# Seven PSUM banks of an attention loop in one ring, taken by a written rank, and another written order for the quads with an output piece

## The chip, the cores and the metric

One core of one Trainium2 chip runs the whole program. The metric is the device time in microseconds (us) of one execution: the median of the runs.

## The reference

A transformer block on 2048 tokens of width 576: multi-query attention with 32 heads of 18 columns that share one K and one V, then an MLP, each behind a LayerNorm with modulation. What the change touches is the attention:

```python
q = (x @ wq).reshape(B, S, H, Dh).transpose(0, 2, 1, 3)   # H = 32, Dh = 18, S = 2048
k = x @ wk                                                # one head, shared
v = x @ wv
scores = einsum("bhqd,bkd->bhqk", q, k) * (Dh ** -0.5)
p = softmax(scores, axis=-1)
o = einsum("bhqk,bkd->bhqd", p, v)
out = o.transpose(0, 2, 1, 3).reshape(B, S, H * Dh) @ wo
```

## The kernel before

The attention is worked in 32 quads (the loop over `n` at the end of the printed code): four heads and 512 tokens each. TensorE, VectorE and ScalarE each run a list of instructions in order; which instruction comes when is written out by hand in the strings `QUAD` (quads 0 to 8) and `QUADW` (quads 9 to 30), one token per step. Quad 31 has an order of its own made from `LAST` and `LASTW`. The tokens:

- `S0`, `S1`: a score matmul (`st_mm`, L931), 512 columns, from the upper (0) or lower (1) 64 rows of the array. It fills one PSUM bank; ScalarE's exp (L933) empties it into `P`. 64 a quad.
- `M0`, `M1`: a matmul (`smax_mm`, L319) whose bank VectorE empties with a maximum (L953), 48 a quad; these prepare the softmax's shift for the quad after. `X1` (L941, emptied by ScalarE's Relu at L944) and `R1` (L319 again, emptied by VectorE at L951) work in pairs, 8 each a quad. So a quad has 128 banks to fill and empty.
- `V1` to `V4`: so many 128-column pieces of P times V (`pv_mm`, L921), with 32 columns of weights in four column tiles; they run eight chunks behind the exps and add up in the one bank `psC`. 64 pieces a quad. What stands between two `V` tokens is called a burst here.
- `F1`, `F2` (`smax_fin1`, `smax_fin2`, L349 to L366): the next quad's maxima are reduced, transposed on TensorE (L357), copied by ScalarE (L359) and VectorE (L360), and written by four DMAs (L364) from SP's queue into the rows of the next quad's `QST` that its score matmuls read: the first two DMAs into the rows of `S0`, the last two into those of `S1`.
- `T1`, `RC`, `T2`, `OS`: the steps of `post_quad` for the quad before. `WO`: one piece of the output projection (`wo_piece`, L723, 14 matmuls of 288 columns) whose bank VectorE adds to `XT` (L727); in eight of the quads five transposes (L155) follow it.

The eight PSUM banks of this stage (`open_ps("2", 4)`) are split by the names `psM` (three banks, taken in turn by M and R), `psB` (four, taken in turn by S, X, F2, WO and the transposes) and `psC` (one). A matmul that takes a bank waits until the engine that reads it has emptied it. The last quads let odd `S` steps take `psM` as well. Two matmuls that follow each other on different row halves start together:

```python
QUADW = """M1 M1 S0 S0 X1 S1 M0 V4 S1 M0 S1 S0 M1 M0 V4 ..."""
t = ps()                                  # st_mm: psB, or psM in the last quads
t = psM()                                 # mx_mm, M and R
```

Of the kernel before, what the change touches and what calls it, by code (L numbers as in the profile page):

```python
# [8 lines left out]
F32 = mybir.dt.float32  # L9
# [11 lines left out]
NQT = NB * NQ  # L21
# [11 lines left out]
def block_kernel(ctx: ExitStack, tc, x, wqkv, wo, w1, b1, w2, b2, c, wmod, ident_in, out):  # L33
# [7 lines left out]
    PS = {}  # L41

    def open_ps(stage, b):

        if PS:
            PS["pool"].__exit__(None, None, None)
        PS["pool"] = tc.tile_pool(name="ps" + stage, bufs=1, space=bass.MemoryType.PSUM,
                                  **({"reuse_waits": "tile"} if PS else {}))
        PS["t"], PS["b"] = PS["pool"].__enter__(), b

    def psA(): return PS["t"].tile([128, 2, 512], F32, name="psA", bufs=2)
    def psM(): return PS["t"].tile([128, 512], F32, name="psM", bufs=3)
    def psB(): return PS["t"].tile([128, 512], F32, name="psB", bufs=PS["b"])
    def psC(): return PS["t"].tile([128, 512], F32, name="psC", bufs=1)

    open_ps("1", 3)
    def big(): return per.tile([128, 10, 512], F32R, name="big", bufs=3)
# [26 lines left out]
    V = pa.tile([128, S // 128, 32], F32, name="V")  # L84
# [267 lines left out]
            ve.tensor_reduce(m[:, :8], mm[:, :8, :], axis=AX.X, op=ALU.max)  # L352
            ve.tensor_reduce(m[:, 8:], mm[:, 8:, :3], axis=AX.X, op=ALU.max)

    def smax_fin2(n):
        p = psB()
        pe.transpose(p[:16, :128], MR.pop(n), ident)  # L357
        ms = pa.tile([16, 2, 128], F32R, name="ms")
        ac.activation(ms[:, 0], p[:16, :128], AF.Copy, scale=-1.0)  # L359
        ve.scalar_tensor_tensor(ms[:, 1], p[:16, :128], -1.0, ms[:, 0].bitcast(F32), op0=ALU.mult, op1=ALU.subtract)  # L360
        for g in range(2):
            for s in range(2):
                r = 64 * g + R3 + s
                sy.dma_start(QST[n][r:r + 1].rearrange("o p (t c) -> o (p t) c", c=128).bitcast(F32),  # L364
                             ms[8 * g:8 * (g + 1), s].bitcast(F32))
# [80 lines left out]
    for tb in range(NB):  # L446
        nz = big() if tb + 1 < NB else None
        for i, m in enumerate((4, 0, 1, 2, 3)):
# [27 lines left out]
            if tb < 2:  # L476
                for _ in range(NSTAT[tb][i]):
                    ln1_stats(*stats.popleft())
                for _ in range(NAPPLY[tb][i]):
                    b, t = applies.popleft()  # L480
# [3 lines left out]
    load_q(2)  # L484
    ph1.__exit__(None, None, None)
    open_ps("2", 4)
    psM(), psC()
    pxp = tc.tile_pool(name="px", bufs=1, reuse_waits="tile")
    px = pxp.__enter__()
    a2 = tc.tile_pool(name="a2", bufs=1, side="right", reuse_waits="tile")  # L490
# [238 lines left out]
    def wo_piece(tb, t, h2, p):  # L729
        wo_mm(tb, t, h2, p, 0, KD)  # L730
        wo_add(tb, t, h2, p)
# [137 lines left out]
    def tail_parts(o, tail, d, e=po):  # L869

        e.tensor_tensor(d, tail[:, 0], tail[:, 1], op=ALU.subtract)
        for x, y in ((o[:, :2], tail), (o[:, 2], d)):
# [8 lines left out]


    LAG = 8
    QUAD = """S0 M0 S1 S1 M0 V3 S0 M1 S1 M0 M1 S0 V3 M0 S1 M1 S0 V2 M0 S1 S1 M0 X1 S0 V4 T1 X1 M0 M1 M0 S1 S0
            V4 S1 RC M0 S1 S0 M0 S0 M1 V3 S0 M1 R1 S1 S0 M0 X1 V3 M0 S1 S1 R1 S0 M0 S1 V3 M0 X1 M0 S0 S1 S0
            M1 V3 M0 S1 S1 M0 S0 R1 S0 V3 R1 S0 S1 M1 S0 M0 X1 V3 M0 S1 M0 S1 S0 S0 R1 V3 M0 X1 S0 M1 S0 M1
            V3 S1 M0 M0 S1 T2 S0 S1 V4 M0 S1 S0 M1 S0 M1 V3 S0 R1 S1 M0 F1 S1 S0 V3 X1 M0 S1 M0 R1 S0 F2 OS
            V4 M0 M1 S0 S1 M0 X1 V4 S1 M0 S1 S0 M1 M0 S1 V2 R1 S0 M1 S0 V2 S0 S1 M0 M1 V2 S1""".split()
    QUADW = """M1 M1 S0 S0 X1 S1 M0 V4 S1 M0 S1 S0 M1 M0 V4 M0 S1 S0 M0 S1 T1 M0 X1 V4 S1 RC S0 S0 M1 M0 S1 V4
            S0 R1 M1 S0 S1 M0 S1 V3 S1 M0 S0 X1 M0 M0 S1 V2 M0 S1 S0 R1 V2 M0 X1 M0 S1 S0 S1 M0 V4 S0 T2 R1  # L890
            M0 S1 OS S0 M1 WO S0 R1 M1 S0 M1 S0 X1 V3 S0 M1 M0 S1 S1 M1 S0 V3 M0 S1 S0 R1 S0 M0 X1 V3 M0 S1
            X1 M0 S1 M0 S1 V4 S1 M0 R1 S0 M1 S0 V4 S0 M1 M0 F1 S1 S0 S1 V4 M0 S1 M0 X1 S0 M1 F2 V4 M1 S0 S0
            S1 M0 S1 M0 V3 R1 S0 S0 S1 R1 M0 V3 S0 S1 M0 S1 M0 S1 V3 M0 S1 M1 S0 M1 S0 V3""".split()
    LASTW = "S0 S1 S0 S1 S0 S1 WO V4 S0 S1 V4".split()
    LAST = "S0 S1 S0 S1 V4 S0 S1 S0 S1 V4".split()
    P, PVt = {}, {}
# [27 lines left out]
            posts.append(post_quad(n, PVt.pop(n)))  # L924
            next(posts[0])

    def st_mm(n, kc, g, i, ps):
        if (n, kc) not in P:
            P[n, kc] = pb.tile([128, 4, TB], F32, name="P", bufs=4)
        t = ps()  # L930
        pe.matmul(t, KS[64 * g:64 * g + 64, 128 * kc:128 * (kc + 1)], QST[n][64 * g:64 * g + 64, i, :],  # L931
                  start=True, stop=True)
        ac.activation(P[n, kc][:, 2 * i + g, :], t, AF.Exp, scale=SCALE)  # L933

    XC = deque()

    def mx_mm(n, u, kb, what, g):
        p, qt = UNITS[u]
        if what == "X":
            t = psB()  # L940
            pe.matmul(t, QST[n][64 * g:64 * g + 64, p, 128 * qt:128 * (qt + 1)], KD1[64 * g:64 * g + 64, :],  # L941
                      start=True, stop=True)
            XC.append(pb.tile([128, 512], F32, name="xc", bufs=2))
            ac.activation(XC[-1], t, AF.Relu)  # L944
            return
        t = psM()
        o = mx_tile(n)[:, 8 * g + 4 * p + qt, (2 if what == "R" else kb):][:, :1]
        smax_mm(n, t, g, p, qt, 3 if what == "R" else kb)
        if what == "R":
            c = XC.popleft()  # L950
            ve.tensor_tensor_reduce(c, t, c, 1.0, -3.0e38, ALU.add, ALU.max, o)  # L951
        else:
            ve.tensor_reduce(o, t, axis=AX.X, op=ALU.max)  # L953
# [13 lines left out]

    pieces = deque((tb, t, h2) for tb in range(NB - 1) for t in range(NT) for h2 in range(2))

    def wo_next(ps):  # L970
        tb, t, h2 = pieces.popleft()
        wo_piece(tb, t, h2, ps())
        for _ in range(2):
            if held[0] == "T":
                held[0] = step(fill)
        if h2 and tb < 2:
            fill.append(ln2_rows(tb, t))

    pq = 0
    for n in range(NQT):  # L980
        ns = [0, 0]
        if n < NQT - 1:
            order = QUADW if n > NQ else QUAD
            if n == NQT - 2:
                order = order + ["WO"]
        else:
            order = []
            for d in range(8):
                order += LASTW + ["RW"] if d == 4 else LAST
                order += {1: ["T1"], 2: ["RC"], 4: ["T2"], 5: ["OS", "V4"]}.get(d, [])  # L990
        if n < NQT - 1:
            kf, kr = (sum(int(tok[1]) for tok in order[:order.index(a)] if tok[0] == "V") // 4 for a in ("F2", "RC"))
            quiet = kf - 2, kf - 1, kr - 1
        for tok in order:
            if tok[0] == "V":
                g = int(tok[1])
                while g:
                    i = min(g, 4 - pq % 4)
                    if pq >= LAG:
                        pv_mm(*divmod((pq - LAG) // 4, 16), pq % 4, pq % 4 + i)  # L1000
                    pq, g = pq + i, g - i
                    if pq % 4 == 0:
                        between(*divmod(pq // 4 - 1, 16))
            elif tok[0] == "S":
                g = int(tok[1])
                st_mm(n, ns[g] // 2, g, ns[g] % 2, psM if ns[g] % 2 and (n == NQT - 1 or n == NQT - 2 and ns[g] > 24) else psB)
                ns[g] += 1
            elif tok in maxima:
                unit = next(maxima[tok], None)
                if unit:  # L1010
                    mx_mm(*unit, tok[0], int(tok[1]))
            elif tok == "WO":
                wo_next(psB)
            elif tok == "RW":
                for i, w in enumerate("hl"):
                    sy.dma_start(WO[w][:, KD - 1, :].bitcast(F32), woscr[i])
            elif tok[0] == "F":
                (smax_fin1 if tok == "F1" else smax_fin2)(n + 1)
            elif n:
                if next(posts[0], 0) == 0:  # L1020
                    posts.pop()
        if n == NQT - 1:
            W1["r"] = per.tile([128, 40, 128], F32R, name="w1a", tag="big", bufs=3)
            load_w1(0, " ".join(OPS) + " tails")
# [13 lines left out]
    def op_pieces(R, e2):  # L1038


        at = {"B11": (0, 0, ve), "B21": (2, 2, e2), "B22": (4, 7, e2), "T2": (6, 5, ve), "T1": (8, 5, ve),
              "T3": (10, 0, ve), "T4": (12, 2, e2), "t0": (0, 4, ve), "t1": (1, 9, ve)}
        less = {"T3": (5, 0, 0), "T4": (2, 5, 2), "T1": (7, 5, 5)}

        def form(what):
            for w in what.split():
                if w[0] == "=":
                    x, y, o = (R[:, i:i + 2] for i in less[w[1:]])
                    (ve if w == "=T3" else e2).tensor_tensor(o, x, y, op=ALU.subtract)
# [455 lines left out]
```

## Time and profile before

| | us |
|---|---|
| median of 3 runs (lowest, highest) | 2227.75 (2227.24, 2228.18) |
| span of the profiled execution | 2225.7 |
| a quad of `QUAD`, from its first score matmul to the next quad's (quad 5) | 37.4 |
| a quad of `QUADW` without transposes (quad 11) | 39.25 |
| a quad of `QUADW` with transposes (quad 12) | 39.9 |
| busy in quad 11: TensorE, VectorE, ScalarE | 39.25, 37.9, 37.3 |

The span runs from the first to the last instruction of the profiled execution; the runs' time has some 2 us around it. The busy times are unions: an instruction's duration overlaps that of its neighbours on the same engine where they are pipelined, and a matmul's end is modelled, so TensorE counts as busy from one start to the next. How fast TensorE really goes is therefore read from the starts of its instructions.

### The profile page before, as it was taken

To read this page: it belongs to the slowest core of one execution; us is meant where nothing else is said; L and a number is where in the kernel's file an instruction comes from. 1 tells how busy PE (TensorE), PEld (TensorE's weight loads), DVE (VectorE), ACT (ScalarE), POOL (GpSimd) and SP (SyncE) were. 2 spreads that over 40 slices of the span, in tenths; PEclk is the share of its full clock that TensorE was granted. 3 is DMA by queue.
4 is the path that set the end of the run, shared out by engine and by line. 5 is a ranking of instruction groups with operands and counts; after the bars stand their busy time and mean duration, and the time that the engine had idled before them with its cause. 6 is when DMAs were issued, how large, how long until landed. Compare 5 with 4: busy or idle time off the path is not lost.

```text
span 2225.7 us, 46108 instructions
## 1 busy us (share of the span) xinstructions
PE 2207.4 (99%) x16630; PEld 1451.2 (65%) x16630; DVE 1931.9 (87%) x3415; ACT 1639.8 (74%) x3145; POOL 1527.0 (69%) x1761
## 2 busy tenths in 40 slices
PE   8999999999999999999999999999999999999999
PEld 6654544444544445454454545888888898989898
DVE  7589999999999999999999983887888878888887
ACT  5569999999999999999999997444444444343443
POOL 6653455666776687677676631888888867877776
PEclk9999999999999999999999999999999999999999
DMA  6232143433333333333333322666666646676664
GB/s 231 85 131 92 34 135 115 139 125 119 127 119 114 115 129 105 107 126 111 126 123 117 115 70 63 205 178 175 178 179 180 185 129 182 180 218 188 177 185 124
DMA packets 184776, 308.00 MB, mean 138 GB/s; under 512 B 19711, under 2 KB 75407, under 8 KB 184549
## 3 DMA queue, kind: packets, MB, share of 16 engines
q1 hardware_dynamic: 184405, 304.91, 44.3%
q8 instruction: 132, 2.16, 0.4%
q14 instruction: 95, 0.78, 0.1%
q10 hardware_dynamic: 144, 0.15, 0.0%
HBM read 200.97 MB, written 93.79 MB: 132 GB/s over the span
## 4 chain that ended last, share of the span: by engine, by line
PE 93%; ACT 1%; DVE 1%; issue 0%; ACTq 0%; DVEq 0%
PE psC L921 24%; PE psB L1144 18%; PE psA L1247 16%; PE psB L931 14%; PE psM L319 12%; PE psB L723 2%; PE psB L941 2%; PE psA L1281 1%; PE psA L723 1%; ACT P L933 1%; PE psB L155 0%; PE psB L248 0%; PE psB L357 0%; PE psM L931 0%; DVE mx L344 0%; DVE mx L337 0%
## 5 line engine op out<-in xcount | busy, mean ns | idle before, releaser
L933 ACT ACTIVATE P<-psB 128x512 f32<-128x512 f32 x2008 | 1051.1, 621 | 43.8 <-PE psM L319 20.0
L953 DVE TENSOR_REDUCE mx<-psM 128x1 f32<-128x512 f32 x1476 | 934.3, 682 | 29.9 <-PE psM L319 12.9
L931 PE MATMUL psB<-qst,KS 64*128 64x512 f32 x2008 | 603.5, 435 | 0.1
L319 PE MATMUL psM<-KS,qst 64*128 64x512 f32 x1722 | 591.2, 435 | 0.5 <-DVE mx L337 0.5
L921 PE MATMUL psC<-P,V 128*32 128x256 f32 (+3 forms) x6600 | 571.9, 440 | 0.5 <-ACT O L738 0.5
L931 PEld LDWEIGHTS psB<-qst,KS 64*128 64x128 f32 x2008 | 300.4, 184 | 225.6 <-ACT P L933 185.1
L319 PEld LDWEIGHTS psM<-KS,qst 64*128 64x128 f32 x1722 | 284.1, 184 | 185.6 <-DVE mx L953 130.2
L1144 PE MATMUL psB<-ops,w1a 128*128 128x512 f32 x1512 | 393.8, 396 | 0.2 <-DVE h L1159 0.2
L1144 PEld LDWEIGHTS psB<-ops,w1a 128*128 128x128 f32 x1512 | 270.1, 188 | 46.7 <-DVE h L1159 0.6
L921 PEld LDWEIGHTS psC<-P,V 128*32 128x32 f32 x6600 | 146.4, 108 | 185.3 <-issue 156.6
L1253 DVE TENSOR_TENSOR XT<-psA,XT 128x576 f32<-128x576 f32 x330 | 241.8, 753 | 18.6 <-PE psA L1247 13.2
L1247 PEld LDWEIGHTS psA<-w2s,big 128*128 128x128 f32 x1584 | 223.0, 188 | 14.0 <-POOL big L1221 2.5
L1247 PE MATMUL psA<-w2s,big 128*128 128x288 f32 x1584 | 230.5, 294 | 0.0
L1157 ACT ACTIVATE psB<-gs 128x512 f32<-128x512 f32 x144 | 86.7, 602 | 127.8 <-DVE gs L1156 127.7
L1221 POOL TENSOR_TENSOR big<-s,big 128x512 fp32r<-128x512 f32 x132 | 170.8, 1294 | 10.6
L951 DVE CUSTOM_DVE_ANT_0 xc<-psM,xc 128x512 f32<-128x512 f32 x246 | 166.3, 683 | 12.8 <-PE psB L931 6.4
L1153 ACT ACTIVATE h<-psB,b1t 128x512 f32<-128x512 f32 x144 | 97.9, 680 | 102.0 <-PE psB L1144 81.3
L758 POOL TENSOR_TENSOR os<-O,os 128x512 fp32r<-128x512 f32 x31 | 39.9, 1286 | 185.4 <-ACT os L757 185.4
L944 ACT ACTIVATE xc<-psB 128x512 f32<-128x512 f32 x246 | 154.7, 629 | 4.0 <-PE psB L941 1.4
L1156 DVE SCALAR_TENSOR_TENSOR gs<-psB,h 128x512 f32<-128x512 f32 x144 | 98.6, 685 | 39.8 <-ACT psB L1154 39.7
L792 POOL TENSOR_TENSOR r<-r,r 128x256 fp32r<-128x256 f32 (+1 forms) x162 | 121.8, 752 | 13.0
L1162 ACT ACTIVATE big<-h 128x512 fp32r<-128x512 f32 x39 | 24.7, 634 | 133.8 <-DVE h L1159 133.8
(212 smaller groups left out, 3326.8 us busy)
## 6 DMA issues: line engine op xcount, KB each, us to landing
w1a<-w1scr SPq DMA_DIRECT2D x252, 256.0 KB
w2s<-w2sum SPq DMA_DIRECT2D x132, 288.0 KB
w1scr<-r SPq DMA_DIRECT2D x126, 256.0 KB
w2s<-w2scr SPq DMA_DIRECT2D x76, 288.0 KB
w2scr<-r SPq DMA_DIRECT2D x72, 288.0 KB
w2sum<-r SPq DMA_DIRECT2D x72, 288.0 KB
qst<-qscr SPq DMA_DIRECT2D x192, 72.0 KB
w1a<-w2scr SPq DMA_DIRECT2D x33, 288.0 KB
```

The costliest lines, as they stand in the source:

```text
L319: pe.matmul(o, QST[n][64 * g:64 * g + 64, p, 128 * qt:128 * (qt + 1)], KS[64 * g:64 * g + 64, 512 * kb:512 * (kb + 1)], start=True, stop=True)
L792: po.tensor_tensor(o[:, n:2 * n], src, o[:, :n].bitcast(F32), op=ALU.subtract)
L921: pe.matmul(PVt[n][32 * j:32 * (j + 1), cs], V[:, kc, :], t[:, j, cs], start=(kc == 0 and h0 == 0), stop=(kc == 15), skip_group_check=True)
L931: pe.matmul(t, KS[64 * g:64 * g + 64, 128 * kc:128 * (kc + 1)], QST[n][64 * g:64 * g + 64, i, :], start=True, stop=True)
L933: ac.activation(P[n, kc][:, 2 * i + g, :], t, AF.Exp, scale=SCALE)
L944: ac.activation(XC[-1], t, AF.Relu)
L951: ve.tensor_tensor_reduce(c, t, c, 1.0, -3.0e38, ALU.add, ALU.max, o)
L953: ve.tensor_reduce(o, t, axis=AX.X, op=ALU.max)
L1144: pe.matmul(o, x, y, start=(first and i == 0), stop=(i == len(terms) - 1), skip_group_check=True)
L1221: po.tensor_tensor(unit(u, 1), x, unit(u, 0).bitcast(F32), op=ALU.subtract)
L1247: pe.matmul(p[:, i, :288], x[:, ts_], W2S[k][:, y], start=(bool(first) and q == 0), stop=(q == 2), skip_group_check=True)
L1253: ve.tensor_tensor(o, p[:, :, :288], o, op=ALU.add)
```

## The change

The three banks of `psM` and the four of `psB` become one list of seven, `RING`. A step takes the bank at place `rank` of that list, and the bank goes to the list's end; rank 0 is the bank that was taken longest ago. The rank stands in the order strings: `S0+` has rank 1, `X1++` rank 2. `psB()` outside of these steps takes rank 0 while the ring exists. In `QUAD` the tokens are the same and stand in the same order, with ranks added (34 plus signs); `QUADW` is another order of the same tokens, with 37.

```diff
-    def psB(): return PS["t"].tile([128, 512], F32, name="psB", bufs=PS["b"])
+    def psB(): return bank() if RING else PS["t"].tile([128, 512], F32, name="psB", bufs=PS["b"])
+    RING = []
+    def bank(rank=0):
+        b = RING.pop(rank)
+        RING.append(b)
+        return PS["t"].tile([128, 512], F32, name="bk%d" % b, bufs=1)
...
     open_ps("2", 4)
-    psM(), psC()
+    RING.extend(range(3))
+    bank(), bank(), bank(), psC()
+    RING[:] = 3, 0, 4, 1, 5, 2, 6
...
-    QUADW = """M1 M1 S0 S0 X1 S1 M0 V4 S1 M0 S1 S0 M1 M0 V4 M0 S1 S0 M0 S1 T1 M0 X1 V4 S1 RC S0 S0 M1 M0 S1 V4
-            S1 M0 S1 M0 V3 R1 S0 S0 S1 R1 M0 V3 S0 S1 M0 S1 M0 S1 V3 M0 S1 M1 S0 M1 S0 V3""".split()
+    QUADW = """S1+ M0 M0 X1 S0 X1 M0 V3 S1 M0 M0+ S1 R1 S0+ V2 M1 S0 M0 S1+ S0 R1+ V3 M0 X1+ S0 S1+ S0+ M1 V4 S0 T1
+            R1 M0+ F1 S1 S0 X1+ V4 M0 S1 M0 S1+ S0+ M1 F2 V3 S0+ R1 S0+ S1 M0 S1 M0 V3 M0 X1 S1 M0+ S1 R1+ S0 V3""".split()
...
-    def st_mm(n, kc, g, i, ps):
+    def st_mm(n, kc, g, i, rank):
-        t = ps()
+        t = bank(rank)
...
-            t = psB()
+            t = bank(rank)
-        t = psM()
+        t = bank(rank)
...
+            rank = tok.count("+")
+            tok = tok.rstrip("+")
-                st_mm(n, ns[g] // 2, g, ns[g] % 2, psM if ns[g] % 2 and (n == NQT - 1 or n == NQT - 2 and ns[g] > 24) else psB)
+                st_mm(n, ns[g] // 2, g, ns[g] % 2, rank)
...
     form = op_pieces(YR[0], ve)
+    RING.clear()
     open_ps("3", 4)
```

Counted over the strings, bursts and `V` tokens of a quad become (a burst that runs over the quad's end is counted whole; slots are starts, with two matmuls on different row halves in one):

| | bursts of 7 banks, 4 slots | of 6, 3 slots | of 4, 2 slots | V4 | V3 | V2 | after F2 to the quad's end |
|---|---|---|---|---|---|---|---|
| `QUAD`, both | 8 | 10 | 3 | 5 | 12 | 4 | |
| `QUADW` before | 10 | 9 | 1 | 9 | 8 | 2 | V4, 7, V3, 6, V3, 6, V3, 6, V3 |
| `QUADW` now | 8 | 12 | 0 | 8 | 10 | 1 | V3, 7, V3, 7, V3 |

Two places of TensorE's list show it. The first is where one quad of `QUADW` ends and the next begins (quads 27 and 28), with the semaphores that each waits for; L931 is a score matmul, L319 a maximum's, L921 P times V, and DMAHW a DMA queue's. Before:

```order
L921 MATMUL psC<-P,V 32x384 x4
L319 MATMUL psM<-KS,qst 128x512 [waits DVE_49] x2
L931 MATMUL psB<-qst,KS 128x512 [waits DMAHW7_49,DMAHW6_49,Activation_49]
L931 MATMUL psB<-qst,KS 128x512 [waits Activation_49]
L941 MATMUL psB<-KD_82,qst 128x512 [waits Activation_49]
L931 MATMUL psB<-qst,KS 128x512 [waits DMAHW1_49,DMAHW0_49,Activation_49]
```

Now (the lines have moved: L941 is the score matmul, L327 the maximum's, L951 the X, L931 P times V):

```order
L931 MATMUL psC<-P,V 32x384 x4
L941 MATMUL bk_18866<-qst,KS 128x512 [waits DMAHW2_49,DMAHW1_49,Activation_49]
L327 MATMUL bk_18869<-KS,qst 128x512 [waits DVE_49]
L327 MATMUL bk_18872<-KS,qst 128x512 [waits Activation_49]
L951 MATMUL bk_18875<-KD_82,qst 128x512 [waits DVE_49]
L941 MATMUL bk_18879<-qst,KS 128x512 [waits DMAHW7_49,DMAHW0_49,Activation_49]
```

The first score matmul of a quad was an `S0` that waits for the first two DMAs of L364; now it is an `S1` that waits for the last two, and it stands first in the quad. A score matmul may wait for VectorE now, and a maximum's for ScalarE.

The second place is in quad 5, inside `QUAD`, with the numbers of the tiles. Before:

```order
L319 MATMUL psM_4300<-KS_80,qst_3665 128x512 [waits DVE_49]
L931 MATMUL psB_4304<-qst_3076,KS_80 128x512 [waits Activation_49]
L931 MATMUL psB_4307<-qst_3076,KS_80 128x512 [waits Activation_49]
L319 MATMUL psM_4310<-KS_80,qst_3665 128x512 [waits DVE_49]
L941 MATMUL psB_4313<-KD1_82,qst_3665 128x512 [waits Activation_49]
L931 MATMUL psB_4317<-qst_3076,KS_80 128x512 [waits Activation_49]
```

Now:

```order
L327 MATMUL bk0_4302<-KS_80,qst_3667 128x512 [waits Activation_49]
L941 MATMUL bk6_4306<-qst_3078,KS_80 128x512 [waits Activation_49]
L941 MATMUL bk4_4309<-qst_3078,KS_80 128x512 [waits DVE_49]
L327 MATMUL bk1_4312<-KS_80,qst_3667 128x512 [waits Activation_49]
L951 MATMUL bk3_4315<-KD1_82,qst_3667 128x512 [waits DVE_49]
L941 MATMUL bk5_4319<-qst_3078,KS_80 128x512 [waits Activation_49]
```

The six steps are the same and stand in the same order; four of them take a bank that the other engine emptied.

## Rows read from the trace of the kernel before

**Rows 1.** The page, parts 1 and 4 (the chain that ended last).
```profile
PE 2207.4 (99%) x16630; PEld 1451.2 (65%) x16630; DVE 1931.9 (87%) x3415; ACT 1639.8 (74%) x3145; POOL 1527.0 (69%) x1761
...
PE 93%; ACT 1%; DVE 1%; issue 0%; ACTq 0%; DVEq 0%
```

**Rows 2.** Windows, quads 5, 11, 29: length; busy PE, PEld, DVE, ACT, POOL; clock.
```profile
318.51:355.90 37.39, 37.39 (x367) 18.51 (x363) 36.53 (x71) 36.99 (x76) 24.60 (x37) 1.00 0.41 133
...
547.67:586.92 39.25, 39.25 (x344) 19.17 (x345) 37.89 (x75) 37.30 (x76) 34.96 (x51) 1.00 0.36 122
...
1259.31:1298.57 39.26, 39.26 (x344) 19.27 (x345) 37.08 (x72) 37.29 (x76) 23.77 (x35) 1.00 0.34 116
```

**Rows 3.** Timeline, PE, quad 28: start, length, line, operation, tile, count.
```profile
1221.00 1.06 PE L921 MATMUL psC<-P,V 128*32 128x512 f32 x8
1221.99 0.49 PE L931 MATMUL psB<-qst,KS 64*128 64x512 f32 x1
...
1222.88 1.06 PE L921 MATMUL psC<-P,V 128*32 128x512 f32 x8
1223.88 0.50 PE L319 MATMUL psM<-KS,qst 64*128 64x512 f32 x1
...
1225.00 1.06 PE L921 MATMUL psC<-P,V 128*32 128x512 f32 x8
1225.99 0.73 PE L931 MATMUL psB<-qst,KS 64*128 64x512 f32 x3
1226.33 0.62 PE L319 MATMUL psM<-KS,qst 64*128 64x512 f32 x2
1226.69 0.50 PE L931 MATMUL psB<-qst,KS 64*128 64x512 f32 x1
1227.12 1.06 PE L921 MATMUL psC<-P,V 128*32 128x512 f32 x8
...
1229.23 0.85 PE L921 MATMUL psC<-P,V 128*32 128x384 f32 x8
1230.01 0.50 PE L931 MATMUL psB<-qst,KS 64*128 64x512 f32 x1
```

**Rows 4.** Timeline of the same place, ScalarE and VectorE.
```profile
1224.57 1.57 ACT L933 ACTIVATE P<-psB 128x512 f32<-128x512 f32 x3
...
1225.62 0.70 DVE L741 STREAM_TRANSPOSE T<-O 128x512 f32<-128x512 f32 x1
...
1226.00 0.63 ACT L944 ACTIVATE xc<-psB 128x512 f32<-128x512 f32 x1
...
1226.25 0.65 DVE L953 TENSOR_REDUCE mx<-psM 128x1 f32<-128x512 f32 x1
```

**Rows 5.** Timeline, quad 10's F2 to the next quad's first score matmul.
```profile
539.01 0.28 PE L357 MATMUL psB<-ident,mxf 128*16 128x128 f32 x1
...
539.22 1.07 PE L921 MATMUL psC<-P,V 128*32 128x512 f32 x8
...
540.13 0.25 ACT L359 ACTIVATE ms<-psB 16x128 fp32r<-16x128 f32 x1
...
540.41 2.79 SPq L364 DMA_DIRECT2D qst<-ms  x4
...
547.67 0.47 PE L931 MATMUL psB<-qst,KS 64*128 64x512 f32 x1
```

**Rows 6.** Timeline, program start: a DMA of 2.5 KB and its reader.
```profile
0.72 0.39 SPq L96 DMA_DIRECT2D ct<-in_c  x1
...
2.59 0.21 ACT L120 ACTIVATE st<-ct 128x5 f32<-128x5 f32 x1 [0.59 <-DMA ct<-in_c]
```

**Rows 7.** Timeline, the output piece of quad 10 and the next score matmul.
```profile
524.27 2.14 PE L723 MATMUL psB<-wos,big 126*128 126x288 f32 x14
...
526.34 0.49 PE L931 MATMUL psB<-qst,KS 64*128 64x512 f32 x1
```

**Rows 8.** Waits, PEld, quad 11: us in total, times, longest.
```profile
PEld psB L931 <- ACT P L933: 6.6, 11, 0.8
```

More of the change, by code (lines that the diff above doesn't have):

```diff
@@ L353, in smax_fin1, with smax_fin2 @@
             ve.tensor_reduce(m[:, 8:], mm[:, 8:, :3], axis=AX.X, op=ALU.max)
-    def smax_fin2(n):
-        p = psB()
+    def smax_fin2(n, rank=0):
+        p = bank(rank) if RING else psB()
         pe.transpose(p[:16, :128], MR.pop(n), ident)
@@ L883, in block_kernel @@
     LAG = 8
[L884 to L888, printed above, removed]
-    QUADW = """M1 M1 S0 S0 X1 S1 M0 V4 S1 M0 S1 S0 M1 M0 V4 M0 S1 S0 M0 S1 T1 M0 X1 V4 S1 RC S0 S0 M1 M0 S1 V4
-            S0 R1 M1 S0 S1 M0 S1 V3 S1 M0 S0 X1 M0 M0 S1 V2 M0 S1 S0 R1 V2 M0 X1 M0 S1 S0 S1 M0 V4 S0 T2 R1
-            M0 S1 OS S0 M1 WO S0 R1 M1 S0 M1 S0 X1 V3 S0 M1 M0 S1 S1 M1 S0 V3 M0 S1 S0 R1 S0 M0 X1 V3 M0 S1
-            X1 M0 S1 M0 S1 V4 S1 M0 R1 S0 M1 S0 V4 S0 M1 M0 F1 S1 S0 S1 V4 M0 S1 M0 X1 S0 M1 F2 V4 M1 S0 S0
-            S1 M0 S1 M0 V3 R1 S0 S0 S1 R1 M0 V3 S0 S1 M0 S1 M0 S1 V3 M0 S1 M1 S0 M1 S0 V3""".split()
+    QUAD = """S0+ M0 S1 S1+ M0 V3 S0 M1 S1+ M0 M1++ S0 V3 M0 S1+ M1 S0+ V2 M0 S1+ S1 M0+ X1 S0+ V4 T1 X1 M0 M1 M0
+            S1 S0 V4 S1 RC M0+ S1 S0 M0+ S0+ M1 V3 S0 M1 R1 S1+ S0 M0+ X1 V3 M0 S1 S1+ R1 S0 M0 S1 V3 M0+ X1 M0
+            S0 S1 S0 M1 V3 M0+ S1 S1+ M0 S0 R1+ S0 V3 R1+ S0 S1 M1 S0 M0 X1 V3 M0+ S1 M0 S1 S0 S0 R1 V3 M0+ X1
+            S0+ M1 S0 M1+ V3 S1 M0+ M0 S1 T2 S0 S1 V4 M0 S1 S0 M1+ S0 M1 V3 S0 R1+ S1 M0 F1 S1 S0 V3 X1 M0 S1 M0
+            R1 S0 F2 OS V4 M0+ M1 S0+ S1 M0+ X1 V4 S1 M0 S1+ S0 M1 M0+ S1 V2 R1 S0 M1 S0+ V2 S0 S1 M0 M1 V2 S1""".split()
+    QUADW = """S1+ M0 M0 X1 S0 X1 M0 V3 S1 M0 M0+ S1 R1 S0+ V2 M1 S0 M0 S1+ S0 R1+ V3 M0 X1+ S0 S1+ S0+ M1 V4 S0 T1
+            M1+ S0 S1 M0 S1+ V4 S1 M0 M1 S0 S1+ M0 V4 S1 M0 S1 S0+ M1 S0 R1 V4 S1 M0 M0 RC X1+ S0 M1+ S1 V3 S0
+            M1 S1+ S0 M0 S1 M0 V3 R1 S1 M0 M1+ S0 S1+ S0 V4 S1 T2 OS M0 X1++ M0 S1+ M0 WO S0 M1 S0 M1 S0 M1 V3
+            S1 S0 M1 S0 M0 X1 V3 S1 M0 M1+ M0 S1+ S0 V4 M0 S1+ S0 S1 S0+ R1+ M0 V4 S0+ S1 M0 M1++ M1 S0+ V3 S0
+            R1 M0+ F1 S1 S0 X1+ V4 M0 S1 M0 S1+ S0+ M1 F2 V3 S0+ R1 S0+ S1 M0 S1 M0 V3 M0 X1 S1 M0+ S1 R1+ S0 V3""".split()
     LASTW = "S0 S1 S0 S1 S0 S1 WO V4 S0 S1 V4".split()
@@ L935, in block_kernel, with mx_mm @@
     XC = deque()
-    def mx_mm(n, u, kb, what, g):
+    def mx_mm(n, u, kb, what, g, rank):
         p, qt = UNITS[u]
         if what == "X":
-            t = psB()
+            t = bank(rank)
             pe.matmul(t, QST[n][64 * g:64 * g + 64, p, 128 * qt:128 * (qt + 1)], KD1[64 * g:64 * g + 64, :],
@@ L968, in block_kernel, with wo_next @@
     pieces = deque((tb, t, h2) for tb in range(NB - 1) for t in range(NT) for h2 in range(2))
-    def wo_next(ps):
+    def wo_next(rank):
         tb, t, h2 = pieces.popleft()
-        wo_piece(tb, t, h2, ps())
+        wo_piece(tb, t, h2, bank(rank))
         for _ in range(2):
@@ L991, in block_kernel @@
         if n < NQT - 1:
-            kf, kr = (sum(int(tok[1]) for tok in order[:order.index(a)] if tok[0] == "V") // 4 for a in ("F2", "RC"))
+            names = [tok[:2] for tok in order]
+            kf, kr = (sum(int(tok[1]) for tok in order[:names.index(a)] if tok[0] == "V") // 4 for a in ("F2", "RC"))
             quiet = kf - 2, kf - 1, kr - 1
         for tok in order:
+            rank = tok.count("+")
+            tok = tok.rstrip("+")
             if tok[0] == "V":
@@ L1010, in block_kernel @@
                 if unit:
-                    mx_mm(*unit, tok[0], int(tok[1]))
+                    mx_mm(*unit, tok[0], int(tok[1]), rank)
             elif tok == "WO":
-                wo_next(psB)
+                wo_next(rank)
             elif tok == "RW":
@@ L1017, in block_kernel @@
             elif tok[0] == "F":
-                (smax_fin1 if tok == "F1" else smax_fin2)(n + 1)
+                smax_fin1(n + 1) if tok == "F1" else smax_fin2(n + 1, rank)
             elif n:
```

## The prediction

> **What bounds the kernel now.** I read the page first: TensorE is busy 99% of the span and holds 93% of the chain that ended last [rows 1]. That alone proves little, since a matmul's end is modelled. So I cut the attention into quads with the windows view [rows 2]: a quad of `QUAD` takes 37.39 us, one of `QUADW` 39.25. In quad 11 VectorE is busy 37.89 us and in quad 29, without LayerNorm work between, 37.08, but both last the same 39.25 us: VectorE's total load doesn't set the period.
>
> What does is seen in TensorE's starts [rows 3]. From a V4's first matmul to the next score matmul it is 0.99 us (1221.00 to 1221.99, 1225.00 to 1225.99), from a V3's 0.78. These repeat to the hundredth. The waits view puts 6.6 us of a quad's weight-load waiting down to ScalarE's exps alone [rows 8]; the reader is to see that most of it costs nothing, because those loads wait while a V still streams. A burst of six banks takes 0.89 us where nothing holds it (1221.99 to 1222.88), one of seven 1.12 (1223.88 to 1225.00). The output piece takes 2.07 [rows 7], F2 0.21 [rows 5].
>
> So I can add up what a `QUADW` quad would take if no bank ever held TensorE. A pair's slot is 1.12 - 0.89 = 0.23 us, so a burst of four is 0.66; 0.21 us per 128-column piece makes a V2 0.57. Before: 10 x 1.12 + 9 x 0.89 + 0.66 = 19.87, plus 9 x 0.99 + 8 x 0.78 + 2 x 0.57 = 16.29, plus 2.28 = 38.44 us. The window says 39.25, so **about 0.8 us a quad is lost to banks** that aren't empty. For `QUAD` the same sum is 36.6 against 37.39.
>
> One such place stands in the rows. The burst at 1225.99 has six banks and takes 1.13 us instead of 0.89: its last score matmul starts at 1226.69 [rows 3], 0.06 us after ScalarE finished the Relu of 1226.00 [rows 4], which held the bank it takes. At that moment the burst's own first five matmuls hold five banks (three S, two M) and VectorE, which lost 0.70 us to a transposition at 1225.62, is still reducing the sixth of the others [rows 4]. No bank of the seven is free. I went through quads 11 to 29 so: six to eight steps a quad start within 0.09 us of the evacuation that they need, and at all but one of them none of the other six banks was empty. The split into three and four is rarely what holds TensorE; the sum of seven is.
>
> **The change part by part.** The order of `QUADW`: 8 x 1.12 + 12 x 0.89 = 19.64 instead of 19.87. The V tokens cover the same 64 pieces in the same 19 tokens: 8 x 0.99 + 10 x 0.78 + 0.57 = 16.29, no difference; one more V is cut in two by a chunk's end, whose four more starts lie inside that V's own stream (if they didn't, 22 short starts are well under 1 us). So -0.23 us a quad in TensorE's own work, 21 quads (9 to 29; quad 30 has hardly any maxima left): **-4.8 us**.
>
> The ring in `QUAD`: nothing moves but banks. I laid the new banks over the old trace: five of the six late steps of a quad would wait for the very same evacuation, one (an M0 at the end) would find its bank 0.08 us earlier, and an S0 that gains 0.25 us has an M1 behind it that loses it. I take -0.05 us a quad, **-0.4 us** for the nine, between -0.2 and +0.1 a quad.
>
> The ring in `QUADW`, with the new order: the 0.8 us of bank waits can fall or grow, and no row shows the new order. Bounds: 0 if all are gone, 0.8 + 0.5 if runs of short V tokens crowd the banks more. A burst of seven and a V3 take 1.90 us for seven banks, 0.272 a bank; the two evacuating engines need about 37.3 to 37.9 us for 128, 0.29 a bank [rows 2], so V3 runs overfill the pool and V4 runs drain it. Before, such runs were three, of three or four bursts; now the longest lies over the quad's end (V3 V3 V3, then V3 V2 V3), and the middle is V4s. I take 0.45 us, nearer to the old value than to none, because the seven banks are as many as before: -0.35.
>
> **The new wait.** F2 has moved from five V tokens before the quad's end to three. Before, 8.66 us lay between F2 and the next quad's first score matmul [rows 5]. Now TensorE's own work there is 0.21 + 3 x 0.78 + 2 x 1.12 = 4.8 us. The maxima have to be through in that time: SP issues the four DMAs from 540.41 on, over 2.79 us [rows 5]. Four in 2.79 are 0.70 apart, which puts the last issue at 542.5, 3.5 us after F2. A small DMA issued at 0.72 was read at 2.59 by an engine that waited for it: 1.87 us [rows 6]. So the last rows land about 5.4 us after F2, and the first step of the new quad is now an `S1`, which needs exactly these. **It waits about 0.6 us** unless TensorE is late anyway. Bounds: 0.1, if both bursts before lose 0.24 us to a bank as the one at 1225.99 did; 1.1, if one more exp stands ahead of ScalarE's copy (three in 1.57 us, some 0.5 a step [rows 4]). Behind the waiting S1 stand two M0 and everything else, since TensorE goes in order; ScalarE and VectorE meanwhile empty banks of the burst before, so they don't starve (seven banks hold about 2 us of their work), and the wait falls at the head of a run that would overfill the pool. I count 0.25 of the 0.6 as paid already by bank waits that vanish there: +0.35.
>
> Sum for a `QUADW` quad: -0.23 - 0.35 + 0.35 = -0.23; 21 quads give -4.8, with `QUAD` -5.2. Quad 31 takes seven banks in turn as before, in effect: nothing. No instruction is added on ScalarE, VectorE, POOL or SP. The profiled execution's span of 2225.7 becomes 2220.5, and with the 2 us that lie between span and median **2222.5**.
>
> **The rivals.**
>
> *The banks hardly hold it any more.* If the new order does what seven flexible banks allow, TensorE runs at its own 38.2 us and loses 0.3 at the quad's start: -0.75 a quad, 2212 us. For: those waits are all short, 0.05 to 0.23. Against: at nearly all of them the pool was full.
>
> *Slower: the maxima's DMAs decide.* The S1 waits its whole 0.6 us, the bank waits stay at 0.8 because the rest of the quad is as crowded: +0.6 - 0.23 = +0.4 a quad, +9 us, 2236, and more with one more exp ahead of the copy. It decides as soon as the wait is longer than what it saves behind it. For: the chain is 5.4 us against 4.8. Against: the run behind it wants the pause.
>
> *Nothing.* Evacuation is what limits. The windows view shows VectorE busy 37.89 of 39.25 us, and behind an output piece of 2.07 us it runs dry; what TensorE saves in slots comes back as waits. 2227.75, between 2225 and 2231. The Trainium skill has this as a rule (TensorEngine Tiling (Array Packing), section PSUM Bottleneck): tiling speeds up TensorE but not the evacuation of PSUM, which may become the bottleneck. By that rule the sum's -0.23 and -0.35 would both be nought. The trace agrees at the late steps, where the pool was full, and not in the period, which didn't follow VectorE's load in quads 11 and 29.
>
> *The ranks don't fit.* In the eight quads with transposes two more banks are taken at rank 0, which turns the ring against the ranks as written; if a plus then points at a full bank each time, 0.6 us in each of the eight: about 2229 on top of my sum.
>
> **How the numbers follow.** A measurement of this kernel tells about 0.2% (4.5 us) from no change. Chances: my forecast 0.34 (its own range 2217 to 2228), waits gone 0.22, DMAs decide 0.20, nothing 0.20, ranks 0.04. Faster by over 0.2% (under 2223.3): half of the forecast, all of the first rival, 0.03 of the others: 0.42. Slower (over 2232.2): 0.20 and 0.03: 0.23. The rest, 0.35, within. The range leaves about a tenth out on each side: 2212 to 2236.
>
> **What would show it.** The page after: TensorE still the chain. Right, if a `QUADW` quad lasts about 39.0 us, if the first score matmul of quads 10 to 30 shows a wait for a DMA of `ms` of 0.4 to 0.7 us, if the late steps in the run behind it are fewer, and if quads 1 to 8 stay at 37.4. Wrong, if quads 1 to 8 change by over 0.2 us (then the split was what held them), if no DMA wait is seen (then landing or arrival is misjudged), or if a `QUADW` quad is under 38.6 us or over 39.5.

## The result and the profile after

The change makes the kernel 0.4% slower: 2236.82 us, median of 5 runs (2234.55 to 2238.79), against 2227.75 beside it; ratio 1.0039, interval 1.0028 to 1.005. The forecast was 2222.5. The profiled execution has a span of 2232.4.

Parts 1 and 4 of the page after, which answer to [rows 1]:

```profile
PE 2203.2 (99%) x16806; PEld 1453.9 (65%) x16806; DVE 1927.3 (86%) x3415; ACT 1646.1 (74%) x3145; POOL 1528.5 (68%) x1761
...
PE 88%; DVE 2%; POOL 2%; DMA 1%; ACT 1%; issue 0%; SPq 0%; DVEq 0%; POOLq 0%; ACTq 0%
```

TensorE still counts as busy 99%, but its share of the chain fell from 93% to 88%, and POOL (2%) and DMA (1%) are new in it. The windows view, with the columns of [rows 2], of quads 5, 11, 12 and 28:

```profile
316.17:353.66 37.49, 37.49 (x365) 18.91 (x362) 36.57 (x71) 37.07 (x76) 24.66 (x37) 1.00 0.41 133
545.63:586.24 40.61, 39.99 (x352) 19.51 (x353) 37.91 (x76) 37.59 (x76) 37.54 (x48) 1.00 0.32 107
586.24:626.50 40.26, 40.05 (x357) 19.83 (x358) 37.64 (x74) 38.12 (x77) 21.59 (x33) 1.00 0.37 124
1226.76:1266.26 39.50, 38.95 (x352) 19.32 (x353) 36.87 (x71) 37.46 (x76) 23.11 (x35) 1.00 0.35 114
```

`QUAD` is where it was (37.49; 37.39 in [rows 2]). In the `QUADW` quads TensorE's busy time is now shorter than the quad: 38.95 of 39.50. Quad 11 lost 1.36 us, quad 12 (with transposes) some 0.35. Quads cut at their first exps, in us (quad 31 to the end of its last exp):

| quads | before | after |
|---|---|---|
| 3 to 8 (`QUAD`), mean | 37.43 | 37.47 |
| 27 to 29 (plain `QUADW`), mean | 39.24 | 39.52 |
| 12, 14 ... 22 (with transposes), mean | 39.89 | 40.26 |
| 11 and 17 | 39.25, 39.27 | 40.60, 40.59 |
| 9 to 30, sum | 869.07 | 878.42 |
| 31 | 34.34 | 33.71 |

The profiled execution after also gained 2.6 us in quad 0, of which the last section tells. The loss lies in quads 9 to 30, and there in three places.

**First, the DMA wait.** TensorE's timeline at the end of quad 28, and SP's below it, the place of [rows 5]:

```profile
1260.75 0.28 PE L365 MATMUL bk<-ident,mxf 128*16 128x128 f32 x1
...
1264.85 0.85 PE L931 MATMUL psC<-P,V 128*32 128x384 f32 x8
1266.26 0.47 PE L941 MATMUL bk<-qst,KS 64*128 64x512 f32 x1 [0.55 <-DMA qst<-ms]
1266.26 0.50 PE L327 MATMUL bk<-KS,qst 64*128 64x512 f32 x1
```

```profile
1262.15 2.84 SPq L372 DMA_DIRECT2D qst<-ms  x4
```

From the last V3 to the new quad's first step it is 1.41 us, where a V3 needs 0.78. From F2 to that step it is 5.51 us; TensorE was there after 4.88. The page's row for L941 and the waits view:

```profile
L941 PE MATMUL bk<-qst,KS 64*128 64x512 f32 x2048 | 597.2, 432 | 10.4 <-DMA qst<-ms 7.9
```

```profile
PE bk L941 <- DMA qst<-ms: 7.9, 13, 1.4
```

The view puts 13 of these pauses down to the DMA; the same pause at the start of quad 28 (0.66 us) it puts down to ScalarE's exp, for which the step waits too. Run 5 decides between the two. The longest, 1.4 us, ends quad 13. SP's row there has four DMAs in 3.66 us instead of 2.84, and the last is issued 4.4 us after F2 instead of 3.6; what held SP up is not shown:

```profile
661.91 3.66 SPq L372 DMA_DIRECT2D qst<-ms  x4
```

**Second, a wait that nobody had on the list.** `RC` (DVE L754), POOL's multiply (L755) and `T2` (L757) are steps of one chain. Two rows of VectorE's lines view, after and then before (L747 there):

```profile
L757 DVE STREAM_TRANSPOSE O<-T 128x512 f32<-128x512 f32 x32 | 22.3, 696 | 2.4 <-POOL T L755 2.4
```

```profile
L747 DVE STREAM_TRANSPOSE O<-T 128x512 f32<-128x512 f32 x32 | 22.1, 691 | 0.0
```

The timeline of quad 11, after, all engines:

```profile
560.60 0.24 DVE L754 RECIPROCAL R<-T 128x16 f32<-128x16 f32 x1
...
565.71 1.05 POOL L755 TENSOR_TENSOR T<-T,R 128x512 f32<-128x512 f32 x1
565.71 2.12 PE L733 MATMUL bk<-wos,big 126*128 126x288 f32 x14
...
566.79 0.71 DVE L757 STREAM_TRANSPOSE O<-T 128x512 f32<-128x512 f32 x1 [1.10 <-POOL T L755]
...
567.54 0.63 ACT L767 ACTIVATE os<-O 128x512 fp32r<-128x512 f32 x1 [1.57 <-DVE O L757]
```

POOL had preparation of weights in its queue and began the multiply 4.9 us after `RC` had ended. VectorE was ready for `T2` 5.1 us after `RC` (560.60 to 565.69); in the same quad of the kernel before it came to it 9.2 us after (554.42 to 563.60). VectorE stood 1.10 us before `T2`, ScalarE 1.57, their banks filled up, and the six-bank burst behind the output piece took 1.99 us (567.77 to 569.76) instead of 0.90. So in quads 11 and 17 (1.10 and 1.00 us before `T2`); quad 23 has 0.25 us of it. That makes the 2.4 us of the row above. Quad 13, 0.8 us longer than other plain quads, has no such wait; its loss is the late fourth DMA.

**Third, the quads with transposes.** VectorE and TensorE at the end of quad 12 (L155 and L156 are here the statistics of a LayerNorm):

```profile
622.60 0.44 DVE L155 BATCH_NORM_STATS2 bst<-XT 128x6 f32<-128x288 f32 x1
623.07 0.21 DVE L156 BATCH_NORM_AGGREGATE mv<-bst 128x2 f32<-128x12 f32 x1
623.20 0.64 DVE L961 CUSTOM_DVE_ANT_0 xc<-bk,xc 128x512 f32<-128x512 f32 x1
```

```profile
623.93 0.49 PE L327 MATMUL bk<-KS,qst 64*128 64x512 f32 x1
...
625.53 0.85 PE L931 MATMUL psC<-P,V 128*32 128x384 f32 x8
626.50 0.46 PE L941 MATMUL bk<-qst,KS 64*128 64x512 f32 x1
```

The last burst takes 1.60 us, where the same burst of quad 28 takes 1.13: VectorE has the 0.6 us of the LayerNorm statistics ahead of it. Runs 9 and 10 test this. The DMA pause behind it is only 0.19 here. Either way the quad starts 5.5 us after F2: the pause hides the late reductions.

### The profile page after: what moved, and what is told of

Read it like the earlier page. It is cut to its first block, busy times and chain, and to the rows that moved or that the text cites. A ratio compares the mean times of both kernels' runs of the same rounds, so it can differ in the third digit from the quotient of the medians.

```text
span 2232.4 us, 46436 instructions
## 1 busy us (share of the span) xinstructions
PE 2203.2 (99%) x16806; PEld 1453.9 (65%) x16806; DVE 1927.3 (86%) x3415; ACT 1646.1 (74%) x3145; POOL 1528.5 (68%) x1761
## 4 chain that ended last, share of the span: by engine, by line
PE 88%; DVE 2%; POOL 2%; DMA 1%; ACT 1%; issue 0%; SPq 0%; DVEq 0%; POOLq 0%; ACTq 0%
PE psC L931 22%; PE psB L1158 18%; PE psA L1261 16%; PE bk L941 15%; PE bk L327 10%; PE bk L733 2%; PE bk L951 2%; PE psA L1295 1%; DMA qst<-ms 1%; DVE mx L963 1%; PE psA L733 1%; POOL r L802 0%; PE psB L256 0%; POOL r L863 0%; PE bk L365 0%
## 5 line engine op out<-in xcount | busy, mean ns | idle before, releaser
L943 ACT ACTIVATE P<-bk 128x512 f32<-128x512 f32 x2048 | 1066.5, 625 | 44.5 <-PE bk L327 18.4
L963 DVE TENSOR_REDUCE mx<-bk 128x1 f32<-128x512 f32 x1476 | 935.0, 682 | 51.5 <-PE bk L327 38.9
L941 PE MATMUL bk<-qst,KS 64*128 64x512 f32 x2048 | 597.2, 432 | 10.4 <-DMA qst<-ms 7.9
L327 PE MATMUL bk<-KS,qst 64*128 64x512 f32 x1722 | 590.1, 437 | 0.9
L931 PE MATMUL psC<-P,V 128*32 128x256 f32 (+3 forms) x6776 | 572.2, 433 | 1.0 <-ACT O L748 1.0
L941 PEld LDWEIGHTS bk<-qst,KS 64*128 64x128 f32 x2048 | 295.0, 184 | 284.0 <-ACT P L943 159.3
L327 PEld LDWEIGHTS bk<-KS,qst 64*128 64x128 f32 x1722 | 271.8, 184 | 130.3 <-ACT P L943 59.2
L931 PEld LDWEIGHTS psC<-P,V 128*32 128x32 f32 x6776 | 152.3, 108 | 192.8 <-issue 158.3
L961 DVE CUSTOM_DVE_ANT_0 xc<-bk,xc 128x512 f32<-128x512 f32 x246 | 167.3, 680 | 2.8 <-PE bk L327 1.7
L954 ACT ACTIVATE xc<-bk 128x512 f32<-128x512 f32 x246 | 151.4, 616 | 0.1
```

Of the source, the lines that this page charges most:

```text
L327: pe.matmul(o, QST[n][64 * g:64 * g + 64, p, 128 * qt:128 * (qt + 1)], KS[64 * g:64 * g + 64, 512 * kb:512 * (kb + 1)], start=True, stop=True)
L931: pe.matmul(PVt[n][32 * j:32 * (j + 1), cs], V[:, kc, :], t[:, j, cs], start=(kc == 0 and h0 == 0), stop=(kc == 15), skip_group_check=True)
```

## The experiments

All were timed beside the kernel before (medians 2227.75, 2227.47 and 2228.18 us beside runs 1 to 4, 5 to 8 and 9 to 10).

### 1. F2 earlier

```diff
-... V4 M0 S1 M0 S1+ S0+ M1 F2 V3 ...
+... V4 M0 S1 F2 M0 S1+ S0+ M1 V3 ...
```

> F2 of QUADW is taken four steps earlier (into the burst behind the V4), nothing else. Theory A, late chains: the first S1 of a quad loses 0.66 us to the DMAs of ms in 21 quads, so about 13.9 us go: 2223 us, a QUADW quad of 38.85 us, V3 to the next quad's S1 back at 0.78 us. Theory B, crowded banks: the pause only stood in for bank waits, which come back: quads of about 39.3, 2232 us or more.

Measured: 2232.57 us (2231.03 to 2235.48), ratio 1.0024 (1.0014 to 1.0033). The DMA wait is gone, and the new quad follows its V3 after 0.78 us. But a plain quad (`QUADW` without transposes; the mean of quads 27 to 29 where no other is named) takes 39.20, only 0.3 less than in the change where the pause was 0.66. That is theory B's time, but not for its reason, as the other bursts take no longer than before the change. F2 now splits a burst, and two bursts of two and four steps with F2 (L365) between take 1.37 us (1258.56 to 1259.93) where one burst and F2 took 1.10:

```profile
1258.56 0.50 PE L941 MATMUL bk<-qst,KS 64*128 64x512 f32 x1
1259.06 0.28 PE L365 MATMUL bk<-ident,mxf 128*16 128x128 f32 x1
...
1259.93 0.42 PE L931 MATMUL psC<-P,V 128*32 128x128 f32 x8
```

The quads with transposes stay at 40.36: without the pause their last burst still takes 1.59.

### 2. RC earlier

```diff
-... S1+ M0 V4 S1 M0 S1 S0+ M1 S0 R1 V4 S1 M0 M0 RC X1+ ...
+... S1+ M0 V4 RC S1 M0 S1 S0+ M1 S0 R1 V4 S1 M0 M0 X1+ ...
```

> RC of QUADW is taken two V4 tokens earlier, nothing else. Theory A: POOL's multiply (L755) is through before T2 in every quad, the 1.0 to 1.1 us extra of quads 11 and 17 and part of 13 and 23 go: 3 to 4 us, about 2233 us, and no wait of DVE O for POOL T. Theory B: the long quads are long for another reason: 2237 us.

`RC` moves over one V4 and ten steps, not over two V4. One thing more moves: the kernel gives POOL no preparation at the place before `RC`, and this place is reckoned from `RC`'s.

Measured: 2233.84 us (2232.35 to 2236.47), ratio 1.0028 (1.0016 to 1.004), 3.0 us less than the change, with ranges that overlap. The trace shows where: quads 11, 17 and 23 are back at 39.51, 39.57 and 39.51, 2.4 us in all. Quad 13 is 0.8 us shorter too, since its fourth DMA is issued in time here, and quads 9 and 18 are 0.4 us longer each. The view of the tile `T` in quad 11 (first start at the end of a row):

```profile
L754 DVE RECIPROCAL R<-T x1: 243/243/243, 558.9 to 558.9; 128x16 f32<-128x16 f32 x1
L755 POOL TENSOR_TENSOR T<-T,R x1: 1047/1047/1047, 564.7 to 564.7; 128x512 f32<-128x512 f32 x1
L757 DVE STREAM_TRANSPOSE O<-T x1: 659/659/659, 567.4 to 567.4; 128x512 f32<-128x512 f32 x1
```

POOL still gets to it 5.6 us late, but `T2` comes after that: what decided was the distance in the order string, as POOL's lateness did not shrink.

### 3. Both

> Both edits. Theory A: the two add up, 2219 us, plain QUADW quads of 38.85 and with transposes of 39.6 us. Theory B: 2230 us or more.

Measured: 2229.38 us (2228.51 to 2232.68), ratio 1.0009 (1.0 to 1.0018). The two gains add, as theory A said (4.25 and 3.0 make 7.25 of the 7.4 measured); its 2219 failed with run 1's 2223.

### 4. The new order without the ring

The kernel before with only `QUADW` replaced, without plus signs: three banks for M and R, four for the rest.

> The kernel before (three banks psM, four psB, its QUAD) with the new order of QUADW and no ring. If the ring has a part in what the new order saves on bank waits, these grow: 0.2 to 0.5 us a quad more than in the changed kernel, 2241 to 2248 us, and quad 0 takes 40.2 us again. If only the order counts, 2237 us, with quad 0 at 40.2 us 2239.

Measured: 2260.22 us (2258.6 to 2263.09), ratio 1.0146 (1.0133 to 1.016). A plain quad takes 40.69 us, 1.17 more than with the ring, over twice the most that was expected; quad 31 is back at 34.34. TensorE in quad 28, and VectorE's R (L951) before it:

```profile
1250.72 0.49 PE L319 MATMUL psM<-KS,qst 64*128 64x512 f32 x1
1250.72 0.72 PE L931 MATMUL psB<-qst,KS 64*128 64x512 f32 x2
1251.32 0.50 PE L319 MATMUL psM<-KS,qst 64*128 64x512 f32 x1
1251.75 0.85 PE L921 MATMUL psC<-P,V 128*32 128x384 f32 x8
```

```profile
1247.44 3.22 DVE L953 TENSOR_REDUCE mx<-psM 128x1 f32<-128x512 f32 x5 [0.72 <-PE psM L319]
1250.58 0.68 DVE L951 CUSTOM_DVE_ANT_0 xc<-psM,xc 128x512 f32<-128x512 f32 x1
```

The maximum's matmul at 1251.32 starts 0.06 us after the R of 1250.58 ended. It needs one of three banks and VectorE has them; the burst takes 1.37 us (from 1250.38), with the ring 1.04. So the split does hold TensorE in this order.

### 5. The four DMAs in the other order

```diff
-        for g in range(2):
+        for g in (1, 0):
             for s in range(2):
                 r = 64 * g + R3 + s
```

> The change, with the four DMAs that write the maxima issued in the other order: the two into the rows of S1 first, the two into the rows of S0 last. Nothing else moves. Theory A (the first step of the new quad, an S1, waits for the last-issued DMA of the chain, and only for that): the last two land some 1.4 us after the first two, so the S1's rows are there before TensorE arrives; the wait passes to the first S0, four steps and 0.46 us later, and shrinks from 0.66 to 0.2 us or less. A plain QUADW quad goes from 39.5 to about 39.1 us, one with transposes by less (its pause hid late reductions), about 2230 in all. Rival B (the S1 is held by something that ends at the same moment, as the bank or the exps behind the copy): no change, 2237. Rival C (the pause was paying for the burst behind it, as the prediction counted 0.25 of 0.6): the pause goes, bank waits of 0.25 come back, a quad falls by 0.2, 2233.

Measured: 2227.88 us (2225.2 to 2230.55), ratio 1.0002 (0.9993 to 1.0011): 8.9 us less than the change, by the order of two pairs of small DMAs. The page's row, and TensorE where quad 28 begins:

```profile
L941 PE MATMUL bk<-qst,KS 64*128 64x512 f32 x2048 | 598.9, 433 | 1.1 <-DMA qst<-ms 0.8
```

```profile
1256.98 0.85 PE L931 MATMUL psC<-P,V 128*32 128x384 f32 x8
1257.76 0.50 PE L941 MATMUL bk<-qst,KS 64*128 64x512 f32 x1
...
1258.39 0.47 PE L941 MATMUL bk<-qst,KS 64*128 64x512 f32 x1
```

The S1 follows its V3 after 0.78 us, and the S0 0.63 later, 0.06 more than in the change. Theory A holds. A plain quad takes 38.99, quad 28 39.01:

```profile
1218.75:1257.76 39.01, 39.01 (x356) 19.16 (x352) 36.88 (x72) 37.50 (x76) 23.09 (x35) 1.00 0.35 115
```

Of the pause's 0.66 us, 0.53 come back, so 0.13 had been paid back by the banks behind it. Quads 12 to 22 with transposes gain 0.12 each, quad 26 0.6, and quad 13, where the fourth DMA had been issued late, 1.4.

### 6. DMA order and RC

> The DMA order of the run before, and RC two V4 earlier as in the second experiment. If the two waits are what the change lost, and independent, the gains add: 2236.8 - 3.0 for RC, and what the DMA order alone gives: about 2227, as fast as the kernel before. If they are not independent (the DMA pause hides POOL's lateness), it stays at the DMA order's own time less 1 or so.

Measured: 2225.25 us (2223.41 to 2226.99), ratio 0.999 (0.9981 to 0.9999). The gains add again: 8.9 and 3.0 make 11.9, measured 11.6. With both waits gone the change's order is no longer slower than the kernel before.

### 7. The quad's head as well

```diff
-S1+ M0 M0 X1 S0 X1 M0 V3 ...
+X1+ M0 M0 S1 S0 X1 M0 V3 ...
```

> As the run before, and the quad's head reads X1+ M0 M0 S1 in place of S1+ M0 M0 X1: the same row halves in the same slots, but the first score matmul comes three steps later, and its S0 follows at once. Theory A: neither S waits for a DMA any more, or under 0.1 us; the last 0.1 to 0.2 us a quad come back: 1 to 3 us less than the run before, about 2224. Rival: the exps start later in the quad (one evacuation less for ScalarE at its head), ScalarE runs dry, and the burst behind waits: nothing gained, or some us lost.

Measured: 2224.63 us (2223.5 to 2226.75), ratio 0.9988 (0.9979 to 0.9997). A plain quad stays at 39.00, so theory A's last 0.1 to 0.2 us a quad aren't there: the score matmuls wait 1.2 us in all for the maxima's DMAs in run 6 and as much here. The 0.6 us against run 6 are within both runs' scatter.

### 8. The ring with the old order

The change, with the old `QUADW`, and 30 plus signs in it that follow the measured ends of the evacuations.

> The kernel of the change (one ring of seven, ranks in QUAD) but QUADW in the old order of the tokens, with 30 plus signs that point each step at the bank whose evacuation ended first in the trace of before. So only the split into three and four goes. The prediction's claim (the split is rarely what holds TensorE): a QUADW quad stays at 39.2 us, 0 to 0.1 less; with quad 31's 0.6, 2226 to 2227.5. Rival (the fourth experiment showed the ring worth 1.1 us a quad for the new order; it is worth 0.3 or more for the old one too): 38.9 us or less, 2221 or less.

Measured: 2226.49 us (2224.72 to 2230.81), ratio 0.9997 (0.9988 to 1.0005). Quads 11 and 28, which answer to [rows 2]:

```profile
547.34:586.61 39.27, 39.27 (x349) 19.04 (x345) 37.87 (x75) 37.30 (x76) 33.88 (x48) 1.00 0.36 121
1220.06:1259.29 39.23, 39.23 (x349) 19.04 (x345) 37.07 (x72) 37.30 (x76) 22.19 (x36) 1.00 0.34 113
```

A plain quad takes 39.24, as before; quad 31 has its 33.71. In the old order the seven flexible banks, with these ranks, are worth nothing.

### 9 and 10. LayerNorm steps later

A LayerNorm step may follow every second group of four V pieces, sixteen groups a quad (`kc`). Run 9 is run 7 with the groups over 12 left out, run 10 with group 1 left out as well (its edit is shown):

```diff
-        if kc % 2 and (held[0] != "T" or not pieces):
+        if kc % 2 and (held[0] != "T" or not pieces) and not (NQ < n < NQT - 1 and (kc > 12 or kc == 1)):
```

> As the run with the changed head, and the LayerNorm steps that are put between the V tokens are left out of the last two places of a quad of QUADW and come two places later, at the next quad's start. Theory A (in the eight quads with transposes the last burst takes 1.59 us instead of 1.13 because VectorE does L155 and L156, 0.6 us, just ahead of the maxima of a run of short V tokens): the last burst falls to 1.2 or less, these quads from 40.15 to about 39.7, 8 x 0.45 = 3.6 us, about 2221. Rival B (the five transposes themselves turn the ring against the ranks, and the late burst is their doing): unchanged, 2224.6. Rival C (the statistics meet the short V tokens of the next quad's start instead): that burst grows by as much, 2224.6.

> As the run before, and the first place of a quad is left out as well, so that the statistics fall between V4 tokens. Theory A: as the run before or up to 1 us less, 2220 to 2221. Rival C of the run before would show here as a gain of 3 us over that run.

Measured: 2225.36 us (2223.59 to 2227.22), ratio 0.9985 (0.9976 to 0.9994), and 2223.17 us (2221.85 to 2223.71), ratio 0.9974 (0.9965 to 0.9984). In both the quads 12 to 22 with transposes fall from 40.15 to 39.73, as theory A of run 9 said. TensorE in run 10 where quad 14 ends:

```profile
701.64 0.50 PE L327 MATMUL bk<-KS,qst 64*128 64x512 f32 x1
...
702.76 0.85 PE L931 MATMUL psC<-P,V 128*32 128x384 f32 x8
703.54 0.50 PE L951 MATMUL bk<-KD,qst 64*128 64x512 f32 x1
```

The last burst is down to 1.12 us. Rival C is right too, in run 9, whose time is that of run 7: the eight quads between (11, 13 ... 25) rise from about 38.97 to between 39.24 and 39.86, as the statistics meet the short V tokens of their start. Run 10 moves them past these, and most of that goes; one quad (15) took 40.56 there, with a DMA wait of 1.5 us. Run 10 beats both kernels, by 0.26% against the one before.

## Why the prediction was wrong

**What bounds the kernel: right.** TensorE's starts, not VectorE's load, set the period; a late place shows in it, less what it saves in the bank waits behind it (0.13 of the pause's 0.66).

**The order's own work (-0.23 a quad): borne out.** A plain quad without the pause (run 5) takes 38.99 us. That is 0.25 less than before. The V tokens take 16.42 us before and 16.41 in run 5, so the one that is cut in two costs nothing.

**The bank waits (0.8 to 0.45): the step that failed.** The new order's own sum is 19.64 + 16.29 + 2.28 = 38.21 us, so run 5 leaves 0.78 for banks, and the old order 39.24 - 38.44 = 0.80. They didn't fall: -0.02, not -0.35. Added up from TensorE's starts, the V tokens hold 0.12 of either figure (16.41 us instead of 16.29), and the bursts, over their shortest times, 0.70 before and 0.68 in run 5. In quad 28 of run 5, 0.50 of this stands in the run of short V tokens over the quad's end, where the prediction saw the pool overfilled: the place was right, the price, taken from a mean over tokens, too low. The largest single loss there, 0.23 us, is at the burst behind the one V2 (1.12 instead of 0.89), as large as that of the burst at 1225.99 in [rows 3]. Why the two orders lose the same in all stays open.

**The DMA wait: mechanism and gross size right, its net size wrong.** Forecast: last rows 5.4 us after F2, TensorE there after 4.8, a wait of 0.6. Measured: 5.5, 4.88, 0.66 (mean of quads 27 to 29). "0.25 counted as paid already" was 0.13, so the term is +0.53 instead of +0.35. With the bank term at -0.02 the sum of a plain quad is -0.23 - 0.02 + 0.53 = +0.28: 39.52, as measured. The Trainium skill (DMA: Bandwidth & Descriptors, section Rules for kernel authors) asks for a DMA to be issued early and its semaphore waited on late. The trace agrees: run 5 issues the two DMAs that are needed first 1.4 us earlier, and that is worth 8.9 us.

**What was not on the list: the wait of `T2` for POOL** (2.4 us in the trace; run 2 takes 3.0 off the median), and the eight quads with transposes, which got +0.37 where the sum had -0.23. The prediction went through the moved F2 and no other moved step. The whole gap between forecast and result is 9.1 + 5.2 = 14.3 us: 13 plain quads by 0.33 (banks) and 0.18 (pause), 6.6; eight quads with transposes by 0.6, 4.8; `T2`, 2.4; the late fourth DMA of quad 13, 0.8; `QUAD`, +0.04 a quad instead of -0.05, 0.8; together 15.4, less 0.6 for quad 31, which is 14.8. The rest is in quads 9, 10 and 15, which lost 0.12 to 0.17 us and not 0.28.

**"The split is rarely what holds TensorE": right for the old order, which it was read off; it doesn't hold for the new.** Run 8 against the kernel before: nothing in a plain quad. The change against run 4: 1.17 us a plain quad. No term of the sum rests on it, but without the ring the new order would have lost 1.5% and not 0.4%.

**Quad 31 (nothing): wrong by a little.** It takes 0.63 us less; runs 4 (34.34) and 8 (33.71) show that the ring does it.

**The rivals.** "The maxima's DMAs decide" named the place, and its 2236 is the result within 1 us, but with a lucky sum: its +0.4 a quad was +0.28 in the plain ones, the rest came from `RC` and the transposes. "The banks hardly hold it any more" falls with the 0.78. "Nothing", by which what TensorE saves in its slots comes back as bank waits, falls too: in run 5 a plain quad is 0.25 us shorter, which is all of the 0.23. By the rule of the Trainium skill named there (TensorEngine Tiling (Array Packing), section PSUM Bottleneck) neither the -0.23 nor the -0.35 would have come. The trace agrees with the second (-0.02) and not with the first. "The ranks don't fit" was given the quads with transposes, and they did lose; but run 10, which moves nothing but statistics, takes 0.43 us a quad off them. They are then 0.73 us longer than the plain quads of the same run, against 0.65 before, so the ranks can have 0.1 us of it at most.

## What to carry to other kernels

When an order of instructions written by hand is changed, list every pair of producer and consumer on different engines whose distance has shrunk (F2 and S1, `RC` and `T2`, the statistics and the next run of reductions), and compare each distance with the longest chain seen between them, other work in the queues included; what is gained in TensorE's list can be lost again at any one of them. Where several small DMAs feed the next stage, issue first the one whose reader stands first: here that alone was worth 8.9 us of 2237. A claim read off one order, as that the split of the banks costs nothing, need not hold for another.

## What the runs showed of the hardware

Four DMAs of one queue were issued 0.7 us apart, and TensorE, which waited for the last, started 1.9 us after its issue (1264.36 to 1266.26); in [rows 6], at the program's start, it was 1.87. It is not always so: at the start of quad 15 in run 10 it was 3.5 (702.31 to 705.78).

Unlooked for was a stretch at the attention's start. The windows view of 130 to 140 us, of the kernel before and then of the change (the number behind the busy times is the granted clock):

```profile
130.00:140.00 10.00, 10.00 (x50) 4.16 (x52) 7.94 (x14) 7.85 (x15) 1.22 (x1) 0.66 0.93 310
```

```profile
130.00:140.00 10.00, 9.86 (x74) 4.29 (x74) 9.72 (x18) 9.65 (x20) 2.06 (x1) 1.00 0.93 322
```

A part of this stretch ran at the lower of TensorE's two levels (1.2 GHz) in one execution and all of it at the higher (2.4 GHz) in the other: quad 0 took 40.24 us before and 37.68 after. Kernels with the same first quads fell on either side (37.94 in run 5, 39.91 in run 6), so it isn't the change's doing. With it the two profiled executions differ by 6.7 us, without it by 9.3; the medians differ by 9.1. What decides it stays open.
